# Gated decode kernel: the output projection matrix in runs of four rows, its operands from one transpose a group

## The chip, the cores and the metric

The kernel runs on one core of a Trainium2 chip. The metric is the device time of one execution in microseconds (us).

## The reference

One decode step of a gated mix of two branches, for a batch of 8 and a width of 576. Everything is bfloat16 at the edges.

```python
x = A_x                                             # [8, 1, 576]
g = sigmoid((x * gate_w).sum(-1, keepdims=True))    # one gate a batch row
# branch A: attention over the last W = 2048 positions of a cache of 8192
q = (x @ wq).reshape(B, 1, 32, 128).transpose(0, 2, 1, 3)
k = repeat(k_cache[:, :, Sk - W:, :], 2, axis=1)    # 16 K/V heads, two query heads each
v = repeat(v_cache[:, :, Sk - W:, :], 2, axis=1)
p = softmax(einsum("bhqd,bhkd->bhqk", q, k) * 128 ** -0.5)
a = einsum("bhqk,bhkd->bhqd", p, v).transpose(0, 2, 1, 3).reshape(B, 1, 4096) @ wo   # wo: [4096, 576]
# branch B: a channel MLP
b = gelu(layernorm(x) @ w1 + b1) @ w2 + b2          # w1: [576, 4608]
return g * a + (1 - g) * b
```

K and V are 2 x 8 x 16 x 2048 x 128 elements, 134 MB; all weights together are some 20 MB.

## The kernel before

**Planner.** The program is written as a list of operations, each with an engine, dependencies and a guessed cost. `schedule()` places them greedily by estimated start time and so fixes one order for each engine; `emit()` then writes that order with semaphore waits. What runs when on the chip is decided by those fixed orders and the waits. All large loads are issued by SP, in one order (`stream`): K units and V units in turn, a load of the projection matrix `wo` after each eighth V unit, and at the end the bias `b2` and the four chunks of `w2`. The loads land in nine slots of 16 KB a partition (`take_slot`, `slot_free`); SP waits until the work on a slot's old contents is done.

**Units and groups.** A group `g` is two K/V heads; there are 8. A unit is half a K/V head: four batch rows, 2048 positions, 2 MB. So a group has four K units and four V units (`q` = 0 to 3).

- `k_unit`: the load (L627), copies on POOL that lay the queries out as block matrices (L635), two 128x2048 transposes on DVE (L642), and QK matmuls on PE (L659 and, with the weights held, L173) into four PSUM banks.
- `softmax(g)` after the group's last K unit: maximum (L587) and small steps on DVE, four exponentials on ACT (L601), four transposes of the probabilities on DVE (L606). Then the row sums: the partial sum of each partition times the 32x32 identity `i32` (`dsum`, L610), a matmul with all ones (L611) that gives each partition all 32 sums in a row, the reciprocal (L613), and the product with the gate in the same layout (`rg`, L618).
- `v_unit`: the load (L675), sixteen PV matmuls on PE (L682) in four column groups, an evacuation on ACT to `EV` in f32 (L691), and four f32 matmuls (L697) that add up the parts: `EV` is the stationary operand (128 columns) and `i32` the moving one (8 columns). The result has the head dimension on partitions and 8 columns a unit. After each second unit ACT copies it out (`o32`, L707) and POOL multiplies by `rg` into `oT` (L715; for the last item DVE does it from PSUM).
- `wo_chunk`: a load of 8 heads of `wo` (L723), one row of 576 a partition and head, in a slot with a pitch of 768; then for each item two times two matmuls (L541) that add to the output accumulator in PSUM, columns 0 to 287 and 288 to 575 in two column groups.
- `m2_chunk`: `w2` (L746), the last chunk in three pieces; its matmuls add to the same accumulator by L541.

At the end DVE and ACT copy the accumulator out, half each (L764, L765), and SP and ACT store it (L767).

**Start.** Queries (L464, L466), the first MLP layer (L498, L500) and the gate's broadcast (L445) run before the first QK; POOL makes identities, masks and selection matrices in that time, and L404 is its one step in the layer norm.

Of the kernel before, what the change touches and what calls it, by code (L numbers as in the profile page):

```python
# [179 lines left out]
def build_kernel(nc, A_x, A_k_cache, A_v_cache, A_wq, A_wo, B_x, B_w1, B_b1, B_w2, B_b2, gate_w, out):  # L180
# [16 lines left out]
    WOP = 768  # L197
# [7 lines left out]
    with ExitStack() as es:  # L205
# [22 lines left out]
        req("i32", 32, F32)  # L228
        req("idf8", 8, F32)
# [19 lines left out]
        req("dsum", 32, F32)  # L249
        req("rr", 32, F32)  # L250
        req("rg", 2 * 32, F32)
        req("o32", 2 * 16, F32)
        req("EV", 2 * 512, F32)
        req("oT", Hkv * 16, BF)
# [54 lines left out]
        dsum = view("dsum")  # L309
        rr = view("rr")  # L310
        rg = view("rg").rearrange("p (g m) -> p g m", g=2)
        o32 = view("o32").rearrange("p (u m) -> p u m", u=2)
        oT = view("oT").rearrange("p (u h b) -> p u h b", u=Hkv, h=2)
# [20 lines left out]
        def col(i, parts=128):  # L334
            return cols[0:parts, i:i + 1]
# [23 lines left out]
        o_idf = add("pool", lambda e: e.tensor_copy(idf8, ident[0:8, 0:8]), deps=[o_ident], name="idf8", cost=0.15)  # L359
        o_nhalf = add("pool", lambda e: e.memset(col(C_NHALF, 8), -0.5), name="nhalf", cost=0.1)  # L360
# [79 lines left out]
        def b1ev_fn(e):  # L440
# [4 lines left out]
        o_gp = add("pe", lambda e: e.matmul(ps[:, BK_X, 384:400], ones_f[0:8, :], dg[:, 0:16], start=True, stop=True),  # L445
                   deps=[o_dga, o_dgb, o_onesf], name="g_pe", cost=0.4, after=[o_yTp])
        o_yT = add("dve", ev_T(yT, 1), deps=[o_gp, o_yTp], name="yT_ev", cost=0.2)
        o_gb = add("dve", lambda e: e.tensor_copy(gb, ps[:, BK_X, 384:400]), deps=[o_gp], name="gb_ev", cost=0.15)
        o_obh = add("dve", lambda e: e.tensor_copy(ob[:, 0:8], dg[:, 8:16]), deps=[o_dgb], name="ob_hi", cost=0.12)
# [4 lines left out]
        for q in range(4):  # L454
            o_i32.append(add("dve", (lambda q=q: lambda e: e.tensor_copy(i32[32 * q:32 * q + 32, :], ident[32 * q:32 * q + 32, 32 * q:32 * q + 32]))(),
                             deps=[o_ident, o_obl], name="i32_%d" % q, cost=0.15, prio=-1))

# [126 lines left out]
        def softmax(g):  # L584
# [25 lines left out]
            ds = add("dve", lambda e: e.tensor_scalar(out=dsum, in0=i32, scalar1=k(S), scalar2=None, op0=ALU.mult), deps=[s_] + o_i32 + ([rg_done[g - 1]] if g else []), name="ds_%d" % g, cost=0.16, prio=5)  # L610
            sp_ = add("pe", lambda e: e.matmul(ps[:, BK_S, 0:32], ones_f, dsum, start=True, stop=True), deps=[ds] + b6_r[-2:], after=b6_w[-1:], name="sum_pe%d" % g, cost=0.5, prio=5)  # L611
            b6_w.append(sp_)
            rc = add("dve", lambda e: e.reciprocal(out=rr, in_=ps[:, BK_S, 0:32]), deps=[sp_], name="rc_%d" % g, cost=0.16, prio=5)  # L613
            b6_r.append(rc)

            def rg_fn(e):
                in1 = bass.AP(arena_f, offset=foffs("gb"), ap=[[AST // 2, 128], [0, 2], [1, 8], [0, 2]])
                return e.tensor_tensor(out=rg[:, g % 2, :].rearrange("p (l b h) -> p l b h", l=2, b=8), in0=rr.rearrange("p (l b h) -> p l b h", l=2, b=8), in1=in1, op=ALU.mult)  # L618
            deps = [rc, o_gb]
            if g >= 2:  # L620
                deps.append(oT_done[2 * (g - 2) + 1])
            rg_done[g] = add("dve", rg_fn, deps=deps, name="rg_%d" % g, cost=0.16, prio=5)
# [48 lines left out]
        def v_unit(i):  # L671
# [21 lines left out]

            def us_fn(e):
                mm = None
                for r in range(4):
                    mm = e.matmul(ps[:, BK_S, OC + 16 * (item % 2) + 8 * (q % 2):OC + 16 * (item % 2) + 8 * (q % 2) + 8], EV[:, i % 2, 128 * r:128 * r + 128], i32[:, 8 * r:8 * r + 8],  # L697
                                  start=(r == 0), stop=(r == 3), skip_group_check=True)
                return mm
            u_sum[i] = add("pe", us_fn, deps=[u_ev[i]] + o_i32 + b6_r[-2:], after=b6_w[-1:], name="us%d" % i, cost=1.0, prio=3)  # L700
            b6_w.append(u_sum[i])
            if q % 2 == 1:
                hl = q // 2
                prev = u_sum[i]
                osrc = ps[:, BK_S, OC + 16 * (item % 2):OC + 16 * (item % 2) + 16]
                if item < Hkv - 1:
                    ev = add("act", lambda e: e.activation(out=o32[:, item % 2, :], in_=osrc, func=ACTF.Copy), deps=[prev] + ([oT_done[item - 2]] if item >= 2 else []), name="oev%d" % item, cost=0.25, prio=3)  # L707
                    o_item_ev[item] = ev
                    b6_r.append(ev)
                    eng, src_, deps = "pool", o32[:, item % 2, :], [ev, rg_done[g]]  # L710
                else:
                    eng, src_, deps = "dve", osrc, [prev, rg_done[g]]

                def om_fn(e):
                    return e.tensor_tensor(out=oT[:, item, :, :].rearrange("p h b -> p b h"), in0=src_.rearrange("p (b h) -> p b h", h=2),  # L715
                                           in1=rg[:, g % 2, 16 * hl:16 * hl + 16].rearrange("p (b h) -> p b h", h=2), op=ALU.mult)
                oT_done[item] = add(eng, om_fn, deps=deps, name="oT%d" % item, cost=0.25, prio=9)

        def wo_chunk(i):
            s = take_slot()  # L720
            h0 = WO_CH * i
            dst = slot(s)[:, 0:WO_CH * WOP].rearrange("p (t c) -> p t c", t=WO_CH)
            d = dma("sp", lambda e: e.dma_start(dst[:, :, 0:D], A_wo[128 * h0:128 * (h0 + WO_CH), :].rearrange("(t p) c -> p t c", p=128)),  # L723
                    "s%d" % s, WO_CH * 128 * D * 2, deps=slot_free[s], name="d_wo%d" % i, after=last_dma[-1:])
            last_dma.append(d)
            ops = []
            for item in range(h0 // 2, (h0 + WO_CH) // 2):
                mms = [(oT[:, item, h, :], dst[:, 2 * item + h - h0, 0:D]) for h in range(2)]
                ops.append(AccGroup("proj%d" % item, mms, [oT_done[item], d], cost=0.5).op)
            slot_free[s] = ops  # L730
# [107 lines left out]
```

## Time and profile before

| | |
|---|---|
| median of 3 runs | 369.37 us (369.34 to 369.59) |
| span of the profiled execution | 367.9 us (the page gives no other time for it) |
| PE, weight loads | 263.5 us busy (72%), 87.0 us (24%) |
| DVE | 210.4 us busy (57%) |
| ACT, POOL | 47.8 us (13%), 37.5 us (10%) |
| moved by DMA | 154.59 MB, 420 GB/s on average |

The profile is one execution, recorded by the hardware profiler. Its span runs from the first to the last instruction; the device time of a run is a little longer. Each row of a view names a source line (L697), an engine, an operation, its tiles and a count. PEld is the weight load of PE. A row of the timeline begins with start and duration in us, and ends with the idle time ahead of it and what ended that. "DMA to landing" is the time from the issue of a load by SP until its last byte has landed. The chain that ended last is followed back from the last instruction to what released it, step by step.

### The profile page before, as it was taken

How to read it: one execution, taken by the hardware profiler on the slowest of the kernel's cores; microseconds unless marked ns; L12 is line 12 of the kernel's file. 1: busy time of each engine (PE TensorE's matmuls, PEld its weight loads, DVE VectorE, ACT ScalarE, POOL GpSimd, SP SyncE). 2: the span in 40 equal slices, each digit the busy share in tenths (PEclk: the TensorE clock that was granted, in tenths of full speed). 3: DMA queues.
4: the chain of work that ended last, by engine and by line, in shares of the span. 5: the costliest groups of instructions: out<-in, count | busy, mean ns of one | idle time of the engine just before them, and what ended most of it. 6: DMA issues, size and time to landing. Idle time of an engine off the chain costs nothing.

```text
span 367.9 us, 4129 instructions
## 1 busy us (share of the span) xinstructions
PE 263.5 (72%) x1837; PEld 87.0 (24%) x1429; DVE 210.4 (57%) x253; ACT 47.8 (13%) x117; POOL 37.5 (10%) x163
## 2 busy tenths in 40 slices
PE   0349984797698589773986399774976398773984
PEld 0339200122132022110321032110321032113542
DVE  0704599699686665459654674469544775364000
ACT  1010000210300220003000310003100300003200
POOL 7020011012011002000101002010110000000000
PEclk9999999699599869887897869886996879886659
DMA  8999999999999999999999999999999999999994
GB/s 345 428 412 424 435 430 433 428 428 428 433 429 431 422 433 426 428 435 427 433 431 433 408 434 432 429 426 433 433 436 428 414 434 424 431 433 440 402 429 193
DMA packets 14923, 154.59 MB, mean 420 GB/s; under 512 B 1292, under 2 KB 5428, under 8 KB 6072
## 3 DMA queue, kind: packets, MB, share of 16 engines
q1 hardware_dynamic: 14848, 154.29, 98.9%
q8 instruction: 13, 0.21, 0.2%
q10 hardware_dynamic: 56, 0.03, 0.0%
q14 instruction: 6, 0.05, 0.0%
HBM read 154.31 MB, written 0.01 MB: 419 GB/s over the span
## 4 chain that ended last, share of the span: by engine, by line
DMA 61%; PE 20%; DVE 16%; SPq 1%; issue 1%; ACT 0%; DVEq 0%; ACTq 0%
DMA arena<-in_A_k_cache_dram 50%; DMA arena<-in_B_w_dram 11%; DVE arena L642 10%; PE ps L173 9%; PE ps L659 3%; DVE arena L587 3%; PE ps L498 2%; PE ps L682 2%; PE ps L697 2%; DVE arena L606 1%; DVE arena L590 1%; PE ps L500 1%; SPq L675 1%; DVE arena L596 0%; SPq L746 0%
## 5 line engine op out<-in xcount | busy, mean ns | idle before, releaser
L642 DVE STREAM_TRANSPOSE arena<-arena 128x2048 f32<-128x2048 f32 x64 | 145.5, 2299 | 71.1 <-DMA arena<-in_A_k_cache_dram 60.1
L173 PE MATMUL ps<-arena 128*128 128x512 bf16 x408 | 141.3, 462 | 0.0
L659 PE MATMUL ps<-arena 128*128 128x512 bf16 x128 | 58.8, 459 | 21.4 <-DVE arena L642 21.3
L691 ACT ACTIVATE arena<-ps 128x512 f32<-128x512 f32 x32 | 19.1, 598 | 196.8 <-PE ps L682 196.8
L659 PEld LDWEIGHTS ps<-arena 128*128 128x128 bf16 x128 | 15.0, 117 | 124.6 <-issue 71.3
L635 POOL COPY arena<-arena 32x32 bf16<-32x32 bf16 x128 | 26.0, 203 | 159.8 <-PE ps L173 145.2
L697 PE MATMUL ps<-arena 128*128 128x8 f32 x256 | 35.3, 269 | 8.7 <-ACT arena L691 7.7
L697 PEld LDWEIGHTS ps<-arena 128*128 128x128 f32 x256 | 34.0, 208 | 21.8 <-ACT arena L691 15.2
L682 PE MATMUL ps<-arena 128*32 128x512 bf16 x512 | 36.4, 410 | 2.9 <-DMA arena<-in_A_v_cache_dram 2.9
L651 PE MATMUL ps<-arena 128*128 128x512 bf16 x8 | 4.7, 585 | 40.8 <-DVE arena L606 40.8
L587 DVE TENSOR_REDUCE arena<-ps 128x1 f32<-128x2048 f32 x8 | 18.3, 2282 | 21.6 <-PE ps L173 21.6
L601 ACT ACTIVATE arena<-ps,arena 128x512 bf16<-128x512 f32 x32 | 21.6, 686 | 40.9 <-DVE arena L596 40.9
L606 DVE STREAM_TRANSPOSE arena<-arena 128x512 bf16<-128x512 bf16 x32 | 19.9, 674 | 0.9 <-ACT arena L601 0.9
L682 PEld LDWEIGHTS ps<-arena 128*32 128x32 bf16 x512 | 11.3, 100 | 37.4 <-issue 27.1
L715 POOL TENSOR_TENSOR arena<-arena 128x16 bf16<-128x16 f32 x15 | 4.0, 266 | 141.7 <-ACT arena L707 141.7
L498 PE MATMUL ps<-arena 128*128 128x8 bf16 x144 | 10.9, 201 | 4.7 <-DMA arena<-in_B_w_dram 4.7
L541 PE MATMUL ps<-arena 128*8 128x288 bf16 (+1 forms) x140 | 11.9, 316 | 2.9 <-DMA arena<-in_B_w_dram 2.8
L498 PEld LDWEIGHTS ps<-arena 128*128 128x128 bf16 x144 | 10.8, 157 | 5.2 <-DMA arena<-in_B_w_dram 5.2
L651 PEld LDWEIGHTS ps<-arena 128*128 128x128 bf16 x8 | 0.9, 107 | 45.1 <-DVE arena L606 45.1
L613 DVE RECIPROCAL arena<-ps 128x32 f32<-128x32 f32 x8 | 2.9, 358 | 13.9 <-PE ps L611 13.9
L420 PE MATMUL ps<-arena 8*128 8x8 bf16 x8 | 0.5, 167 | 13.4 <-DVE arena L393 9.7
L715 DVE TENSOR_TENSOR arena<-ps,arena 128x16 bf16<-128x16 f32 x1 | 0.2, 229 | 16.7 <-PE ps L697 16.7
(83 smaller groups left out, 97.1 us busy)
## 6 DMA issues: line engine op xcount, KB each, us to landing
arena<-in_A_k_cache_dram SPq DMA_DIRECT2D x32, 2048.0 KB, 33.3
arena<-in_A_v_cache_dram SPq DMA_DIRECT2D x32, 2048.0 KB, 34.1
arena<-in_B_w_dram SPq DMA_DIRECT2D x1, 4608.0 KB, 24.3
arena<-in_A_wo_dram SPq DMA_DIRECT2D x4, 1152.0 KB, 36.6
arena<-in_A_wq_dram SPq DMA_DIRECT2D x1, 4096.0 KB, 13.0
arena<-in_B_w_dram SPq DMA_DIRECT2D x3, 1296.0 KB, 14.8
arena<-in_B_w_dram SPq DMA_DIRECT2D x2, 576.0 KB, 20.6
arena<-in_A_wq_dram SPq DMA_DIRECT2D x1, 512.0 KB, 3.6
```

The lines of the kernel that those rows point to most:

```text
L173: return e.add_instruction(mybir.InstMatmult(name=nc.get_next_instruction_name(), engine=mybir.EngineType.PE, ins=[e.lower_ap(rhs), e.lowe ...
L498: ins = e.matmul(out_, lhsT, yT[:, kt, :], start=(kt == 0), stop=False)
L541: ins = e.matmul(ps[32 * j:32 * j + 8, BK_ACC, 0:JN], lhsT, rhs[:, JN * j:JN * j + JN], start=False, stop=True, skip_group_check=True, til ...
L587: mx = add("dve", lambda e: e.tensor_reduce(out=k(MX), in_=ps[:, 0:4, :].rearrange("p a n -> p (a n)"), axis=AXL.X, op=ALU.max), deps=[qk_ ...
L601: return e.activation(out=Pm[:, 512 * c:512 * c + 512], in_=ps[:, c, :], func=ACTF.Exp, bias=k(NB), scale=SCALE, accum_out=k(SUM + c))
L606: pts.append(add("dve", (lambda c=c: lambda e: e.transpose(bass.AP(arena, offset=aoffs("PT") + 2048 * (g % 2) + 128 * c, ap=[[AST, 128], [ ...
L635: return e.tensor_copy(dst, src)
L642: tr = add("dve", (lambda h=h, kb=kb: lambda e: e.transpose(bass.AP(arena_f, offset=foffs("KT") + kb * 2048, ap=[[AST // 2, 128], [1, 2048]]),
L659: mm = e.matmul(*args, start=False, stop=last) if rc == 0 else held_matmul(nc, e, *args, stop=last)
L682: mm = e.matmul(ps[c:c + 32, BK_OS[i % 2], :], PT[:, g % 2, 512 * q + 32 * t:512 * q + 32 * t + 32], slot(s)[:, 512 * t:512 * t + 512], st ...
L691: u_ev[i] = add("act", lambda e: e.activation(out=EV[:, i % 2, :], in_=ps[:, BK_OS[i % 2], :], func=ACTF.Copy), deps=[prev] + ([u_sum[i - ...
L697: mm = e.matmul(ps[:, BK_S, OC + 16 * (item % 2) + 8 * (q % 2):OC + 16 * (item % 2) + 8 * (q % 2) + 8], EV[:, i % 2, 128 * r:128 * r + 128 ...
```

## The change

Four matrix rows that lie together in `wo` now go to one partition. A load of 8 heads is two groups of 128 partitions x 4 rows: partition `p` of group `t` gets rows `4 p` to `4 p + 3`, 4608 B in one piece. The contraction of the projection is thereby split in another way: its 512 rows of a group (4 query heads x 128) are taken as `4 p + j`, with four matmul pairs for `j` = 0 to 3 in place of one pair a head.

The left operands have to follow. The sum of the units is turned round: a fixed selection matrix `selu` (64 columns) is stationary and `EV` (128 columns) moves, so that the result has query head and batch row on partitions (a block of 32 for each of the group's 4 heads, in it the 8 batch rows four times over) and the head dimension along the row. The row sums come from one matmul with a selection matrix `seln` and one moving column, so that each partition has its own sum; reciprocal and gate product are 128x1. ACT scales each partition while it copies the group out (`on`, bf16), and one 32x32-block transpose on DVE a group gives `oT` with `4 p + j` as the order. POOL builds `selu`, `seln` and `r8` once at the start, and one more small matmul gives the gate by partition (`gcol`).

Line numbers in the changed kernel: K transposes L663, QK L680, PV L703, evacuation L712, sums L721, row sums L638, reciprocal L640, gate product L642, scaling L727, group transpose L730, projection and MLP matmuls L569.

```diff
-            ds = add("dve", lambda e: e.tensor_scalar(out=dsum, in0=i32, scalar1=k(S), ...
-            sp_ = add("pe", lambda e: e.matmul(ps[:, BK_S, 0:32], ones_f, dsum, start=True, stop=True), ...
+            sp_ = add("pe", lambda e: e.matmul(ps[:, BK_S, 0:1], seln, k(S), start=True, stop=True), deps=[s_] + o_seln + ...
-            rc = add("dve", lambda e: e.reciprocal(out=rr, in_=ps[:, BK_S, 0:32]), ...
+            rc = add("dve", lambda e: e.reciprocal(out=rr, in_=ps[:, BK_S, 0:1]), ...
-            rg_done[g] = add("dve", rg_fn, deps=deps, name="rg_%d" % g, cost=0.16, prio=5)
+            rg_done[g] = add("dve", lambda e: e.tensor_tensor(out=rg[:, g % 2:g % 2 + 1], in0=rr, in1=gcol, op=ALU.mult), ...
...
+            hl = q // 2
+            osl = ps[64 * hl:64 * hl + 64, BK_S, OC + 128 * (g % 2):OC + 128 * (g % 2) + 128]
                 for r in range(4):
-                    mm = e.matmul(ps[:, BK_S, OC + 16 * (item % 2) + 8 * (q % 2):...], EV[:, i % 2, 128 * r:128 * r + 128], i32[:, 8 * r:8 * r + 8],
-                                  start=(r == 0), stop=(r == 3), skip_group_check=True)
+                    mm = e.matmul(osl, selu[:, r, q % 2, :], EV[:, i % 2, 128 * r:128 * r + 128],
+                                  start=(q % 2 == 0 and r == 0), stop=(q % 2 == 1 and r == 3), skip_group_check=True, tile_position=(0, 64 * hl))
...
-                    ev = add("act", lambda e: e.activation(out=o32[:, item % 2, :], in_=osrc, func=ACTF.Copy), ...
-                oT_done[item] = add(eng, om_fn, deps=deps, name="oT%d" % item, cost=0.25, prio=9)
+            if q == 3:
+                o_item_ev[g] = add("act", lambda e: e.activation(out=on[:, g % 2, :], in_=ps[:, BK_S, OC + 128 * (g % 2):OC + 128 * (g % 2) + 128], func=ACTF.Copy, scale=rg[:, g % 2:g % 2 + 1]), ...
+                oT_done[g] = add("dve", lambda e: e.transpose(bass.AP(arena, offset=aoffs("oT") + 128 * g, ap=[[AST, 128], [1, 128]]),
+                                                              bass.AP(arena, offset=aoffs("on") + 128 * (g % 2), ap=[[AST, 128], [1, WOR], [WOR, 32]])), ...
...
-            dst = slot(s)[:, 0:WO_CH * WOP].rearrange("p (t c) -> p t c", t=WO_CH)
-            d = dma("sp", lambda e: e.dma_start(dst[:, :, 0:D], A_wo[128 * h0:128 * (h0 + WO_CH), :].rearrange("(t p) c -> p t c", p=128)),
+            NT = WO_CH // WOR
+            dst = slot(s)[:, 0:WO_CH * D].rearrange("p (t j c) -> p t j c", t=NT, j=WOR)
+            d = dma("sp", lambda e: e.dma_start(slot(s)[:, 0:WO_CH * D].rearrange("p (t c) -> p t c", t=NT), A_wo[128 * h0:128 * (h0 + WO_CH), :].rearrange("(t p j) c -> p t (j c)", p=128, j=WOR)),
...
-            for item in range(h0 // 2, (h0 + WO_CH) // 2):
-                mms = [(oT[:, item, h, :], dst[:, 2 * item + h - h0, 0:D]) for h in range(2)]
+            for t in range(NT):
+                g = h0 // WOR + t
+                mms = [(oT[:, g, j, 0:8], dst[:, t, j, :]) for j in range(WOR)]
...
+        o_r8 = add("pool", lambda e: e.tensor_copy(r8..., ...idf8...), deps=[o_idf], name="r8", cost=0.2)
+        o_su0 = add("pool", lambda e: e.memset(view("selu"), 0.0), name="selu0", cost=0.5)
+        def g_fn(e):
+            e.matmul(ps[:, BK_X, 384:400], ones_f[0:8, :], dg[:, 0:16], start=True, stop=True)
+            return e.matmul(ps[:, BK_X, 400:401], r8, col(C_G, 8), start=True, stop=True)
+                    o_selu.append(add("pool", fn, deps=o_i32 + [o_su0], ...))     # 16 copies
+                o_seln.append(add("pool", fn, deps=o_i32, ...))                   # 4 copies
```

More of the change, by code (lines that the diff above doesn't have):

```diff
@@ L699, in us_fn @@
                 return mm
-            u_sum[i] = add("pe", us_fn, deps=[u_ev[i]] + o_i32 + b6_r[-2:], after=b6_w[-1:], name="us%d" % i, cost=1.0, prio=3)
+            u_sum[i] = add("pe", us_fn, deps=[u_ev[i]] + o_selu + b6_r[-2:], after=b6_w[-1:], name="us%d" % i, cost=1.0, prio=3)
             b6_w.append(u_sum[i])
[L702 to L716, printed above, removed]
-                oT_done[item] = add(eng, om_fn, deps=deps, name="oT%d" % item, cost=0.25, prio=9)
@@ new lines, in v_unit @@
+            if q == 3:
+                o_item_ev[g] = add("act", lambda e: e.activation(out=on[:, g % 2, :], in_=ps[:, BK_S, OC + 128 * (g % 2):OC + 128 * (g % 2) + 128], func=ACTF.Copy, scale=rg[:, g % 2:g % 2 + 1]),
+                                   deps=[u_sum[i], rg_done[g]] + ([oT_done[g - 2]] if g >= 2 else []), name="oev%d" % g, cost=0.3, prio=9)
+                b6_r.append(o_item_ev[g])
+                oT_done[g] = add("dve", lambda e: e.transpose(bass.AP(arena, offset=aoffs("oT") + 128 * g, ap=[[AST, 128], [1, 128]]),
+                                                              bass.AP(arena, offset=aoffs("on") + 128 * (g % 2), ap=[[AST, 128], [1, WOR], [WOR, 32]])),
+                                 deps=[o_item_ev[g]], name="oT%d" % g, cost=0.25, prio=9)
```

64 lines of the change are left out of this document (41 added, 23 removed).

## The prediction

> **What bounds the kernel now.** I read the page's span, DMA line and queue table first, then the chain that ended last, then busy time by stretch, and last the PE rows behind the final transfers.
>
> ```profile
> span 367.9 us, 4129 instructions
> ...
> DMA  8999999999999999999999999999999999999994
> ...
> DMA packets 14923, 154.59 MB, mean 420 GB/s; under 512 B 1292, under 2 KB 5428, under 8 KB 6072
> ...
> q1 hardware_dynamic: 14848, 154.29, 98.9%
> q8 instruction: 13, 0.21, 0.2%
> ...
> arena<-in_A_wo_dram SPq DMA_DIRECT2D x4, 1152.0 KB, 36.6
> ```
>
> The 16 DMA engines are at nine tenths or more in every slice but the first and the last: the kernel is a stream of 154 MB, and PE, DVE, ACT and POOL work beside it. The four loads of the output projection matrix are 4.7 MB of that stream. Each brings 8 heads x 128 rows of 576 bf16, so 1024 pieces of 1152 B; the four make 4096 of the 5428 packets under 2 KB. A load is listed 36.6 us before it lands: the queue is deep.
>
> ```profile
> 291.28 29.20 DMA arena<-in_A_k_cache_dram
> ...
> 348.46 16.55 DMA arena<-in_B_w_dram
> 365.02 0.04 issue
> 365.06 0.43 PE ps L541 x4
> ```
>
> In the chain the last K load lands at 320.5 (291.28 + 29.20) and the last piece of the second MLP matrix at 365.0. Four matmuls, the copy out and the store are all that follows. So what counts is how fast the bytes pass, and whether PE is ready when the last ones land.
>
> **The change, part by part.** Terms are taken off the profiled span of 367.9 us. The page gives no other time for that execution; the median of the runs, 369.37 us (369.34 to 369.59), is 1.47 us above it, and I leave that gap as it is.
>
> *The transfers.* Columns below: stretch, its length, busy time of PE, weight loads, DVE, ACT and POOL, PE clock, DMA share, GB/s.
>
> ```profile
> 140.00:200.00 60.00, 43.42 (x269) 11.62 (x189) 35.72 (x33) 6.93 (x17) 6.49 (x31) 0.86 1.01 431
> 220.00:285.00 65.00, 49.14 (x286) 12.64 (x196) 37.77 (x33) 7.11 (x18) 6.74 (x32) 0.85 1.01 431
> 124.00:138.00 14.00, 7.87 (x46) 2.64 (x33) 10.68 (x22) 3.98 (x10) 0.21 (x1) 0.76 1.02 421
> 205.00:219.00 14.00, 7.88 (x50) 2.04 (x36) 11.39 (x21) 3.68 (x10) 0.81 (x4) 0.76 1.03 422
> 286.00:300.00 14.00, 7.87 (x46) 1.70 (x37) 11.32 (x21) 3.38 (x9) 0.82 (x4) 0.76 1.03 424
> ```
>
> The first two stretches carry K and V only, in pieces of 16 KB, at 431 GB/s. The other three hold one projection load each and run at 421, 422 and 424. Lost against 431: 14 x (10, 9 and 7)/431 = 0.32, 0.29 and 0.23 us, 0.28 on average. I put that loss to the number of pieces. Per DMA engine a load is 64 pieces of 1152 B, where 73.7 KB in 16 KB pieces would be 4.5; so 0.28 us / 59.5 = 4.7 ns a piece. After the change an engine moves 16 pieces of 4608 B a load (four matrix rows that lie together, for one partition): 48 fewer, 48 x 4.7 ns = 0.226 us a load, **0.90 us for four**. The ends: the rounding of the rates puts a piece between 3.9 and 5.5 ns, so 0.75 to 1.06 us; all of the loss would be 4 x 0.28 = 1.1 us, nothing at all if the loss has another cause than the count. I take 0.90, since the pieces are the one thing that sets these stretches apart.
>
> [...]
>
> *The DMA queue.*
>
> ```profile
> 95.74 0.59 SPq L723 DMA_DIRECT2D arena<-in_A_wo_dram  x1
> 107.98 18.53 SPq L627 DMA_DIRECT2D arena<-in_A_k_cache_dram  x1
> ...
> DMA to landing us min/median/max: 20.1/33.3/40.5
> DVE arena L642 <- DMA arena<-in_A_k_cache_dram: 60.1, 15, 10.5
> ```
>
> The K load behind a projection load takes 18.53 us to issue where that load itself took 0.59; with a quarter of the pieces ahead of it I expect that hold to go. That buys nothing: the shortest way of a K load from issue to landing is 20.1 us (third row), so the engines never ran out of work. Cost 0.
>
> *The sums on PE.*
>
> ```profile
> L697 PE MATMUL ps<-arena 128*128 128x8 f32 x48 | 9.3, 327 | 1.9 <-ACT arena L691 1.4 <-DVE arena L613 0.5
> L541 PE MATMUL ps<-arena 128*8 128x288 bf16 (+1 forms) x92 | 8.4, 331 | 2.9 <-DMA arena<-in_B_w_dram 2.8
> ...
> 337.48 3.49 PEld L697 LDWEIGHTS ps<-arena 128*128 128x128 f32 x16 [0.65 <-issue]
> 337.51 3.55 PE L697 MATMUL ps<-arena 128*128 128x8 f32 x16 [0.54 <-DVE arena L613]
> 340.99 3.38 PE L682 MATMUL ps<-arena 128*32 128x512 bf16 x32
> ...
> 344.30 1.95 PE L697 MATMUL ps<-arena 128*128 128x8 f32 x16
> ...
> L697 PE MATMUL ps<-arena x256: 170/256/382, 76.3 to 353.8; 128*128 128x8 f32 x128
> L611 PE MATMUL ps<-arena x16: 190/273/419, 71.3 to 336.6; 128*128 128x32 f32 x16
> ```
>
> A unit's sum is four f32 matmuls, eight instructions. Today 128 columns are loaded as weights and 8 are streamed; sixteen instructions take 3.55 us at the low clock and 1.95 at the high one, so 0.222 or 0.122 each, and weight load and matmul span the same time. The change turns this round: 64 columns are loaded, 128 streamed. A streamed column costs (190 - 170)/24 = 0.83 ns at best and (419 - 382)/24 = 1.54 ns at worst (last two rows: 32 columns against 8), so 128 cost 0.107 or 0.197 us, and half a load 0.061 or 0.111. If the load hides behind the matmul ahead of it, an instruction costs the larger, 0.107 or 0.197: PE gains a little, nothing lost. If it does not, 0.168 or 0.308. I take the hidden case, because in the two L697 rows that start at 337.5 loads and matmuls lie over each other for all 3.5 us.
>
> Over the span this is beside the DMA. Where it could matter is the tail: after 325 us six units are summed in 9.3 us, and the last matmuls (second row) wait 2.8 us for transfers. That is PE's slack. It grows by the softmax steps that go, and shrinks by the one projection load that falls after the last K landing (0.23):
>
> ```profile
> L691 ACT ACTIVATE arena<-ps 128x512 f32<-128x512 f32 x32 | 19.1, 598 | 196.8 <-PE ps L682 196.8
> L707 ACT ACTIVATE arena<-ps 128x16 f32<-128x16 f32 x15 | 2.8, 184 | 29.6 <-PE ps L697 29.6
> L606 DVE STREAM_TRANSPOSE arena<-arena 128x512 bf16<-128x512 bf16 x32 | 19.9, 674 | 0.9 <-ACT arena L601 0.9
> L610 DVE TENSOR_SCALAR arena<-arena 128x32 f32<-128x32 f32 x8 | 1.9, 242 | 0.3
> L613 DVE RECIPROCAL arena<-ps 128x32 f32<-128x32 f32 x8 | 2.9, 358 | 13.9 <-PE ps L611 13.9
> ```
>
> The multiply at L610 goes (0.24) and the reciprocal reads one column instead of 32 (some 0.2 less). At the very end a group's scaling on ACT comes to about 0.28 us (between 184 ns for 16 columns and 598 for 512) and the transpose to 0.17 to 0.67 (a quarter of L606, or all of it); before, one DVE multiply stood there. Eight matmuls of the group before run meanwhile. I book 0.4 against 0.4: slack stays 2.8 - 0.2, or 2.6 us. The projection itself stays at 64 matmul pairs of the same shape.
>
> *The new wait on DVE.* A group's products were formed on POOL; now DVE stands before the group's 128x128 transpose until ACT has scaled the sums, with K transposes queued behind it, then QK on PE, then SP, which waits for the slot. Each of the seven waits inside the stream is bounded by one evacuation, one sum and one scaling, 0.6 + 1.8 + 0.3 = 2.7 us, and below by nothing. I book 0: DVE stands 60 us waiting for K landings anyway (last row of the queue's fence), and the DMA queue behind it is 20 us deep or more. Without that cover it would be up to 7 x 2.7 = 19 us.
>
> *The start.* Twenty small copies, a copy into a broadcast matrix and a memset join POOL; one f32 matmul joins PE.
>
> ```profile
> 14.75 0.56 POOL L404 TENSOR_TENSOR arena<-arena 8x1 f32<-8x1 f32 x1 [7.12 <-DVE arena L403]
> 24.12 4.12 POOL L635 COPY arena<-arena 32x32 bf16<-32x32 bf16 x16 [8.82 <-ACT arena L483]
> PE ps L498 <- DMA arena<-in_B_w_dram: 4.7, 1, 4.7
> ```
>
> Twenty copies at 4.12/16 = 0.26 us are 5.2 us inside an idle stretch of 8.82; the memset and the broadcast go ahead of a wait of 7.12; PE waits 4.7 us for the first MLP matrix after the queries. Cost 0; if a selection copy spilled past its cover, some 0.3 us on work that the queue hides too.
>
> Sum: 367.9 - 0.90 = 367.0 us of span, **368.5 us** with the 1.47. What a measurement of this kernel can tell is about 0.2%, 0.74 us.
>
> **The rivals.**
> *PE's tail becomes the end (slower).* If weight loads stand in line and the sums stay at the low clock, six units cost 6 x 8 x 0.308 = 14.8 us, 5.5 more than 9.3. Less the 2.6 of slack, the end comes 2.9 us after the forecast: 371.4. It decides from about 9.3 + 2.6 + 0.9 + 0.7 = 13.5 us for the six. For it: the same sixteen instructions show both rates within 10 us. Against it: overlapping loads, and 32 PV matmuls in 3.38 us, eight sets of four in 0.42 each with all their loads inside. [...]
>
> *The engines end apart (either sign).*
>
> ```profile
> 362.00:363.00 1.00, 1.00 (x18) 0.65 (x18) 0.00 (x0) 0.00 (x0) 0.00 (x0) 1.00 0.66 257
> 363.00:364.00 1.00, 0.85 (x12) 0.27 (x8) 0.00 (x0) 0.00 (x0) 0.00 (x0) 1.00 0.38 141
> 364.00:365.00 1.00, 0.54 (x6) 0.18 (x6) 0.00 (x0) 0.00 (x0) 0.00 (x0) 1.00 0.13 48
> ```
>
> The engines finish over some three microseconds, and the slowest sets the end. One of the 13 instruction packets (16 KB, 0.6 us at 431/16 GB/s) on another engine moves the end by 0.6 us: 369.1, or 367.9. For it: the new program has other lengths. Against it: it has about as many instructions.
>
> *The rows do not come as longer pieces, or the loss was not theirs:* 369.4. Against it: source and destination are both 4608 B in one run.
>
> **How the numbers follow.** Forecast 0.60 (its own range 368.2 to 368.7; 0.14 of it under 0.2%); engines apart 0.22, half each way (0.08 faster, 0.14 the same); PE's tail 0.12, slower; no effect 0.06 (0.04 the same, 0.02 slower). Faster 0.46 + 0.08 = 0.54, same 0.14 + 0.14 + 0.04 = 0.32, slower 0.14. The range runs from 367.7, the earlier end with 0.2 to spare, to 369.6, no effect with as much; it leaves out the tail rival.
>
> **What would show it.** Packets fall by 3072 to about 11850, those under 2 KB by 4096 to about 1330. Stretches with a projection load rise to about 429 GB/s. The K issue behind such a load falls to some 0.6 us. The six last sums stay near 9 us, and the last matmuls still wait for transfers by 2 us or more. Wrong: a last PE group that no longer waits for a DMA, a DMA share under 0.9 before 360 us, or a rate at the projection loads that stays at 422.

## Result, and the profile after

| | before | after |
|---|---|---|
| median of 21 runs each, same chip | 369.48 us (369.28 to 369.71) | 368.67 us (368.48 to 369.43) |
| ratio | | 0.9982 [0.9976, 0.9988] |
| profiled execution | span 367.9 us | 369.14 us, span 367.4 us |

The change gains 0.81 us by the medians. The ratio lies near that of the means, 368.83 against 369.49 us, a gain of 0.65. After's 21 executions lie in two groups: 13 at 368.48 to 368.69 us with a mean granted clock of 0.882 to 0.896, and 8 at 369.10 to 369.43 with 0.870 to 0.879. Before's 21 do not split. The profiled execution of after, 369.14 us, is one of the later group, so its tail must be read as that of the eight. What makes the two groups is the one thing that the forecast lacked.

The page of after (span, DMA share in 40 slices, packets):

```profile
span 367.4 us, 4082 instructions
...
DMA  8999999999999999999999999999999999999994
...
DMA packets 11850, 154.58 MB, mean 421 GB/s; under 512 B 1292, under 2 KB 1332, under 8 KB 3000
```

3073 packets are gone, and those under 2 KB are down by 4096, as forecast; the bytes are the same to 0.01 MB. The DMA engines are still at nine tenths or more in every slice but the first and the last. The same five stretches of after (length, busy time of PE, weight loads, DVE, ACT, POOL, PE clock, DMA share, GB/s):

```profile
140.00:200.00 60.00, 43.13 (x255) 10.73 (x180) 35.85 (x33) 6.74 (x15) 4.91 (x24) 0.86 1.01 430
220.00:285.00 65.00, 45.88 (x295) 12.40 (x215) 36.81 (x34) 7.71 (x17) 5.73 (x28) 0.90 1.01 430
124.00:138.00 14.00, 8.69 (x53) 2.50 (x39) 9.28 (x21) 2.99 (x9) 0.82 (x4) 0.76 1.01 428
205.00:219.00 14.00, 7.62 (x40) 2.19 (x22) 11.52 (x21) 3.38 (x9) 0.67 (x4) 0.76 1.02 430
286.00:300.00 14.00, 7.61 (x38) 1.78 (x25) 11.05 (x21) 3.38 (x9) 0.82 (x4) 0.76 1.00 426
```

With a projection load the rate was 421, 422 and 424; it is now 428, 430 and 426, near the 430 of K and V alone. SP's queue of after, the landing of K loads, and two waits of DVE:

```profile
96.22 0.59 SPq L739 DMA_DIRECT2D arena<-in_A_wo_dram  x1
108.31 0.54 SPq L648 DMA_DIRECT2D arena<-in_A_k_cache_dram  x1
...
DMA to landing us min/median/max: 25.1/34.5/42.5
...
DVE arena L663 <- DMA arena<-in_A_k_cache_dram: 57.2, 16, 10.0
DVE arena L730 <- ACT arena L727: 25.9, 7, 11.4
```

The K issue behind a projection load takes 0.54 us instead of 18.53. The new wait on DVE (last row: sum, times, longest) is 25.9 us in seven; a K load takes 25.1 us or more from issue to landing. Groups of PE after 325 us, then its timeline there:

```profile
L721 PE MATMUL ps<-arena 128*64 128x128 f32 x48 | 8.4, 342 | 1.8 <-ACT arena L712 1.4 <-DVE arena L640 0.4
L569 PE MATMUL ps<-arena 128*8 128x288 bf16 (+1 forms) x92 | 10.2, 396 | 2.6 <-DMA arena<-in_B_w_dram 2.6
```

```profile
336.76 3.64 PE L721 MATMUL ps<-arena 128*64 128x128 f32 x16 [0.35 <-DVE arena L640]
342.30 1.96 PE L721 MATMUL ps<-arena 128*64 128x128 f32 x16
352.16 3.74 PE L569 MATMUL ps<-arena 128*8 128x288 bf16 x38
357.74 2.33 PE L569 MATMUL ps<-arena 128*8 128x288 bf16 x18 [1.84 <-DMA arena<-in_B_w_dram]
360.85 4.15 PE L569 MATMUL ps<-arena 128*8 128x288 bf16 x36 [0.78 <-DMA arena<-in_B_w_dram]
```

Sixteen turned-round instructions take 3.64 and 1.96 us (3.55 and 1.95 before), the six sums 8.4 us (9.3). The last two rows are the surprise. Beside them the same matmuls of before:

```profile
354.14 4.29 PE L541 MATMUL ps<-arena 128*8 128x288 bf16 x38
358.83 1.27 PE L541 MATMUL ps<-arena 128*8 128x288 bf16 x18 [0.40 <-DMA arena<-in_B_w_dram]
361.93 2.01 PE L541 MATMUL ps<-arena 128*8 128x288 bf16 x26 [1.82 <-DMA arena<-in_B_w_dram]
364.34 0.54 PE L541 MATMUL ps<-arena 128*8 128x288 bf16 x6 [0.41 <-DMA arena<-in_B_w_dram]
365.06 0.41 PE L541 MATMUL ps<-arena 128*8 128x288 bf16 x4 [0.18 <-DMA arena<-in_B_w_dram]
```

After takes 2.33 us for the 18 where before took 1.27, and 4.15 us for the last 36 with no wait inside, where before waited three times for transfers. The chain that ended last says the same:

```profile
282.49 36.96 DMA arena<-in_A_k_cache_dram
...
329.05 31.75 DMA arena<-in_B_w_dram
...
360.85 4.17 PE ps L569 x36
```

Before, it held transfers until 365.02 and then four matmuls. In this execution it leaves the transfers at 360.8, and PE sets the end.

### The profile page after: what moved, and what is told of

It is laid out like the page before. It is cut to its first block, busy times and chain, and to the rows that moved or that the text cites. A ratio compares the mean times of both kernels' runs of the same rounds, so it can differ in the third digit from the quotient of the medians.

```text
span 367.4 us, 4082 instructions
## 1 busy us (share of the span) xinstructions
PE 255.2 (69%) x1817; PEld 83.4 (23%) x1431; DVE 208.7 (57%) x253; ACT 48.0 (13%) x110; POOL 37.3 (10%) x170
## 4 chain that ended last, share of the span: by engine, by line
DMA 67%; PE 17%; DVE 13%; issue 1%; ACT 1%; SPq 1%; DVEq 0%; ACTq 0%
DMA arena<-in_A_k_cache_dram 51%; DMA arena<-in_B_w_dram 15%; DVE arena L663 11%; PE ps L173 8%; PE ps L526 2%; PE ps L680 2%; PE ps L569 1%; DVE arena L615 1%; PE ps L721 1%; PE ps L703 1%; ACT arena L629 1%; PE ps L528 1%; DVE arena L624 0%; DVE arena L618 0%; SPq L395 0%
## 5 line engine op out<-in xcount | busy, mean ns | idle before, releaser
L663 DVE STREAM_TRANSPOSE arena<-arena 128x2048 f32<-128x2048 f32 x64 | 145.3, 2296 | 62.9 <-DMA arena<-in_A_k_cache_dram 57.2
L173 PE MATMUL ps<-arena 128*128 128x512 bf16 x402 | 135.5, 448 | 17.7 <-DVE arena L663 10.4
L680 PE MATMUL ps<-arena 128*128 128x512 bf16 x114 | 51.5, 452 | 13.3 <-DVE arena L663 13.3
L712 ACT ACTIVATE arena<-ps 128x512 f32<-128x512 f32 x32 | 19.2, 599 | 203.8 <-PE ps L703 203.8
L721 PE MATMUL ps<-arena 128*64 128x128 f32 x256 | 36.5, 291 | 9.6 <-ACT arena L712 7.7
L680 PEld LDWEIGHTS ps<-arena 128*128 128x128 bf16 x128 | 13.9, 109 | 120.5 <-issue 67.9
L703 PE MATMUL ps<-arena 128*32 128x512 bf16 x512 | 34.1, 382 | 3.3 <-DMA arena<-in_A_v_cache_dram 3.3
L721 PEld LDWEIGHTS ps<-arena 128*64 128x64 f32 x256 | 29.2, 144 | 25.4 <-ACT arena L712 14.0
L672 PE MATMUL ps<-arena 128*128 128x512 bf16 x6 | 3.5, 586 | 37.9 <-DVE arena L634 31.8
L703 PEld LDWEIGHTS ps<-arena 128*32 128x32 bf16 x512 | 11.4, 96 | 39.4 <-issue 26.4
L730 DVE STREAM_TRANSPOSE arena<-arena 128x128 bf16<-128x128 bf16 x8 | 2.6, 319 | 26.0 <-ACT arena L727 25.9
L569 PE MATMUL ps<-arena 128*8 128x288 bf16 (+1 forms) x140 | 14.1, 358 | 2.6 <-DMA arena<-in_B_w_dram 2.6
L526 PEld LDWEIGHTS ps<-arena 128*128 128x128 bf16 x144 | 10.8, 159 | 4.7 <-DMA arena<-in_B_w_dram 4.7
L672 PEld LDWEIGHTS ps<-arena 128*128 128x128 bf16 x8 | 0.9, 107 | 46.1 <-DVE arena L634 39.5
L569 PEld LDWEIGHTS ps<-arena 128*8 128x8 bf16 (+1 forms) x140 | 6.7, 102 | 12.5 <-issue 4.2
L640 DVE RECIPROCAL arena<-ps 128x1 f32<-128x1 f32 x8 | 1.4, 169 | 13.9 <-PE ps L638 13.9
## 6 DMA issues: line engine op xcount, KB each, us to landing
arena<-in_A_k_cache_dram SPq DMA_DIRECT2D x32, 2048.0 KB, 34.5
```

The lines of the kernel that those rows point to most:

```text
L173: return e.add_instruction(mybir.InstMatmult(name=nc.get_next_instruction_name(), engine=mybir.EngineType.PE, ins=[e.lower_ap(rhs), e.lowe ...
L526: ins = e.matmul(out_, lhsT, yT[:, kt, :], start=(kt == 0), stop=False)
L569: ins = e.matmul(ps[32 * j:32 * j + 8, BK_ACC, 0:JN], lhsT, rhs[:, JN * j:JN * j + JN], start=False, stop=True, skip_group_check=True, til ...
L663: tr = add("dve", (lambda h=h, kb=kb: lambda e: e.transpose(bass.AP(arena_f, offset=foffs("KT") + kb * 2048, ap=[[AST // 2, 128], [1, 2048]]),
L680: mm = e.matmul(*args, start=False, stop=last) if rc == 0 else held_matmul(nc, e, *args, stop=last)
L703: mm = e.matmul(ps[c:c + 32, BK_OS[i % 2], :], PT[:, g % 2, 512 * q + 32 * t:512 * q + 32 * t + 32], slot(s)[:, 512 * t:512 * t + 512], st ...
```

## The experiments

Theory: the gain is the number of pieces, and PE's clock over the last matmuls takes part of it back in some executions. Rivals: the gain comes from the sums and the softmax steps, or from where a piece begins in memory, or the new waits cost something. All times are medians; before's in the same comparison stands in brackets.

**The pieces alone.** The kernel before with four-row pieces, all else as it was.

```diff
-            dst = slot(s)[:, 0:WO_CH * WOP].rearrange("p (t c) -> p t c", t=WO_CH)
-            d = dma("sp", lambda e: e.dma_start(dst[:, :, 0:D], A_wo[...].rearrange("(t p) c -> p t c", p=128)),
+            dst = slot(s)[:, 0:WO_CH * D].rearrange("p (t c) -> p t c", t=WO_CH)
+            d = dma("sp", lambda e: e.dma_start(slot(s)[:, 0:WO_CH * D].rearrange("p (t c) -> p t c", t=2), A_wo[...].rearrange("(t p j) c -> p t (j c)", p=128, j=4)),
```

> The kernel before with one thing changed: a load of the projection matrix comes in pieces of four rows (4608 B). The sums, softmax and scaling stay as before, so the projection multiplies rows and operands that do not belong together; only its time is read. Theory (number of pieces): 48 pieces fewer an engine and load at 4.7 ns, 0.90 us for four loads: 368.6 us against 369.5 for before, stretches with a projection load at 429 GB/s instead of 421 to 424, the K load behind one issues in about 0.6 us instead of 18. Rival (the gain of the change comes from its compute part): 369.5, no change.

368.61 us (368.48 to 368.72, 8 runs) [369.50]; ratio 0.9975 [0.9965, 0.9985]. Run once more it gave 368.53 (368.36 to 368.85, 8 runs) [369.54], 0.9974 [0.9964, 0.9984]. So 0.89 and 1.01 us, and no second group.

> The runs-only kernel with pieces of four rows once more, as the partner of the eight-row one and of the kernel before with filled tail: 368.6 us.

Stretches and the end of PE in the first of the two:

```profile
124.00:138.00 14.00, 8.95 (x50) 3.23 (x39) 9.79 (x22) 3.57 (x10) 0.27 (x1) 0.76 1.01 431
205.00:219.00 14.00, 8.24 (x46) 3.19 (x38) 10.83 (x22) 3.66 (x10) 0.00 (x0) 0.76 1.01 428
286.00:300.00 14.00, 7.87 (x48) 2.43 (x31) 10.94 (x22) 3.98 (x10) 0.41 (x2) 0.76 1.00 424
```

```profile
355.77 7.05 PE L541 MATMUL ps<-arena 128*8 128x288 bf16 x82
363.27 1.08 PE L541 MATMUL ps<-arena 128*8 128x288 bf16 x10 [0.45 <-DMA arena<-in_B_w_dram]
```

The whole gain is there without any of the arithmetic of the change, and the last ten matmuls still wait for a transfer. A rate over 14 us is coarse, though: in the third stretch the second run of the same program had 433 GB/s where this one has 424.

The packet records of the traces are finer. They give each packet's end, so the packets of the load queue (q1), added up, tell when the same number of bytes had landed in two kernels. Against before's profile, four-row pieces gain 0.23 us at each of the four projection loads in both runs of this kernel, and over the K and V loads between them the difference moves by 0.02 us at most. The kernel after gains 0.24, 0.22, 0.22 and 0.28 us; the 0.05 more at the last also stands in the kernel with the arithmetic alone (next), which gains 0.01 us at most at the others. So the transfers gain at these loads and not between them, and 0.23 us / 48 is 4.8 ns a piece.

**The arithmetic alone.** The kernel after with one-row pieces again.

```diff
-            d = dma("sp", ... slot(s)[:, 0:WO_CH * D].rearrange("p (t c) -> p t c", t=NT), A_wo[...].rearrange("(t p j) c -> p t (j c)", p=128, j=WOR)),
+            d = dma("sp", ... slot(s)[:, 0:WO_CH * D].rearrange("p (t c) -> p t c", t=WO_CH), A_wo[...].rearrange("(t p) c -> p t c", p=128)),
```

> The changed kernel with one thing undone: a load of the projection matrix comes in pieces of one row (1152 B) again; turned sums, scaling by partition and transposes stay. Rows and operands of the projection do not belong together; only the time is read. Theory (number of pieces): 369.5 us, as before, stretches with a projection load at 421 to 424 GB/s, the K load behind one held for some 18 us again. Rival (compute part): 368.6, the whole gain without the pieces. Second rival (the compute part costs, the pieces gain more than 0.9): over 369.7.

369.89 us (369.27 to 370.36, 11 runs) [369.50]; ratio 1.0012 [1.0003, 1.0021]. In its profile the rate and the hold of the K issue are back:

```profile
107.80 18.24 SPq L648 DMA_DIRECT2D arena<-in_A_k_cache_dram  x1
```

```profile
124.00:138.00 14.00, 8.70 (x53) 2.51 (x39) 9.12 (x20) 3.38 (x9) 0.82 (x4) 0.76 1.02 421
```

So the arithmetic gains nothing; it costs 0.4 us, which the forecast had put at nothing and only the second rival of this run had named. The profiled execution was the shortest of the eleven, so its rows do not show where the cost lies. The next two kernels narrow it down.

**PE kept busy before the last chunks.** The kernel after, and the kernel with the arithmetic alone, each with six matmuls on constants ahead of the second chunk of `w2` and four ahead of the third.

```diff
+    WARM = {1: 6, 2: 4}
+                if ci in WARM:
+                    def warm(e, k=WARM[ci]):
+                        for _ in range(k):
+                            ins = e.matmul(ps[:, 0, :], ident, maskR, start=True, stop=True)
+                        return ins
+                    o_m2.append(add("pe", warm, deps=exp_done[NG - 1], ..., after=o_m2[-1:] + [pv_last[NG - 1]]))
```

> The changed kernel with ten matmuls more on PE that nobody reads (128x512, identity times a constant mask, into a free bank): six ahead of the second chunk of the second MLP matrix, four ahead of the third, where PE otherwise waits for transfers. Eight of 21 executions of the changed kernel took 369.1 to 369.4 us at a mean granted clock up to 0.879, the others 368.5 to 368.7 at 0.882 and more. Theory (clock): in those eight PE is granted half its clock over the last matmuls and is later than the last transfer; with the gaps filled the clock stays up, all executions take 368.4 to 368.7, and the last group of matmuls waits for a transfer. Rival (the DMA engines end further apart in some executions): a third of the executions still take 369.1 to 369.4. Second rival (the filling itself delays the last matmuls): 369 and more in all.

> The sums-only kernel (turned sums, pieces of one row; the projection's rows and operands do not belong together, only the time is read) with the ten matmuls that nobody reads ahead of the second and third chunk of the second MLP matrix. The sums-only kernel took 369.3 to 370.4 us, median 369.9, where before took 369.5. Theory (its excess is PE's clock over the last matmuls): 369.3 to 369.6 us, as narrow as before. Rival (the excess lies elsewhere, in transfers or waits): median 369.9 again, and as wide.

With the change: 368.55 us (368.43 to 368.87, 8 runs) [369.50], 0.9975 [0.9965, 0.9985]. With the arithmetic alone: 369.45 (369.29 to 369.59, 11 runs) [369.48], 0.9999 [0.9990, 1.0008]. No execution of the first lies above 368.87, where 8 of 21 did without the filling, and the 0.4 us of the second are gone: nine of its eleven executions without the filling were later than all eleven with it. The mean clocks of these two sets overlap, however (0.873 to 0.888 without, 0.879 to 0.888 with), so that this cost is PE's clock is argued from what removes it. The end of PE with the change and the filling, where L771 is the filling:

```profile
357.18 1.24 PE L771 MATMUL ps<-arena 128*128 128x512 bf16 x5 [0.16 <-issue]
358.35 1.27 PE L570 MATMUL ps<-arena 128*8 128x288 bf16 x18
359.56 1.04 PE L771 MATMUL ps<-arena 128*128 128x512 bf16 x4
361.03 1.88 PE L570 MATMUL ps<-arena 128*8 128x288 bf16 x26 [0.44 <-DMA arena<-in_B_w_dram]
363.36 1.09 PE L570 MATMUL ps<-arena 128*8 128x288 bf16 x10 [0.44 <-DMA arena<-in_B_w_dram]
```

The 18 take 1.27 us and the last 36 wait twice for transfers: the DMA sets the end. What the filling does is shown by the times: this one profiled execution need not have lost its clock without it, since its clock changes, at 349.42 and 356.25 us, lie within 0.1 us of those of an execution of after that kept it (below). Between the two filled kernels only the pieces differ: 369.45 - 368.55 = 0.90 us, though they ran in two comparisons.

**The kernel after once more**, unchanged, for a profile of the earlier group.

> The changed kernel once more, beside the others on one chip. Theory (clock): two groups of executions again, near 368.6 and near 369.2 us, the later one with the lower mean clock. Rival (the first measurement's later group belongs to its chip): one group near 368.6.

368.66 us (368.44 to 369.37, 11 runs) [369.48], 0.9982 [0.9973, 0.9991]; 7 at 368.44 to 368.73 with a clock of 0.882 to 0.893, 4 at 368.96 to 369.37 with 0.875 to 0.882, so here the two groups touch in clock. Its profiled execution (368.55 us, clock 0.888) is of the earlier group:

```profile
352.85 4.18 PE L569 MATMUL ps<-arena 128*8 128x288 bf16 x38
357.75 1.27 PE L569 MATMUL ps<-arena 128*8 128x288 bf16 x18 [0.72 <-DMA arena<-in_B_w_dram]
360.87 2.03 PE L569 MATMUL ps<-arena 128*8 128x288 bf16 x26 [1.84 <-DMA arena<-in_B_w_dram]
363.35 1.08 PE L569 MATMUL ps<-arena 128*8 128x288 bf16 x10 [0.46 <-DMA arena<-in_B_w_dram]
```

The same program, starting the 18 at 357.75 against 357.74: 1.27 us here, 2.33 there, and then 26 in 2.03 and a wait where the other has 36 in 4.15 and none. What differs is the granted clock (the third column from the right). First the profile of after, then this one, in stretches of 1 us:

```profile
350.00:351.00 1.00, 0.46 (x4) 0.46 (x5) 0.00 (x0) 0.49 (x1) 0.00 (x0) 0.93 1.02 430
...
354.00:355.00 1.00, 0.98 (x15) 0.36 (x12) 0.00 (x0) 0.00 (x0) 0.00 (x0) 0.86 1.10 467
355.00:356.00 1.00, 0.90 (x16) 0.45 (x10) 0.00 (x0) 0.00 (x0) 0.00 (x0) 1.00 1.00 425
356.00:357.00 1.00, 0.00 (x0) 0.00 (x0) 0.00 (x0) 0.00 (x0) 0.00 (x0) 1.00 1.02 435
357.00:358.00 1.00, 0.26 (x4) 0.15 (x6) 0.00 (x0) 0.00 (x0) 0.00 (x0) 0.85 0.97 410
...
364.00:365.00 1.00, 1.00 (x12) 0.41 (x8) 0.00 (x0) 0.00 (x0) 0.00 (x0) 0.74 0.00 0
```

```profile
349.00:350.00 1.00, 1.00 (x16) 0.21 (x8) 0.00 (x0) 0.00 (x0) 0.00 (x0) 0.66 1.05 441
...
356.00:357.00 1.00, 1.00 (x16) 0.47 (x11) 0.00 (x0) 0.00 (x0) 0.00 (x0) 0.93 1.07 456
```

The clock is 1.00 or 0.50 in the rows between, so a mixed value tells when it changed: 0.93 in 350 to 351, going down, is 0.14 us at half, so 350.86. In the same way after changes at 350.86 (down), 354.28 (up), 357.70 (down) and 364.52 (up), the other at 349.32 (down) and 356.14 (up). These points lie 3.42, 3.42 and 6.82 us apart, and 6.82: always whole steps of 3.41. The steps of the two executions lie 1.54 us apart. In after the step from 354.28 to 357.70 takes in nearly all of the 1.84 us wait and only 1.60 us of matmuls, and the clock falls at its end, right as the 18 begin. In the other the step from 356.14 to 359.55 has 0.89 + 1.27 = 2.16 us of matmuls and the next one 2.03, and the clock stays. So in these two it is where the steps happen to lie against PE's waits.

**The filling on the kernel before.**

```diff
+    WARM = {1: 6, 2: 4}
+                if ci in WARM:
...
```

> The kernel before with the ten matmuls that nobody reads in the tail. Theory (before ends with its last transfer, whatever PE's clock): 369.5 us, no change. Rival (the filling helps any kernel): 369.3 or less; second rival (it delays the last matmuls): over 369.7.

369.70 us (369.43 to 371.14, 12 runs) [369.54]; 1.0009 [1.0000, 1.0018]. No gain, and two of the twelve are late, as the second rival has it. The profiled execution is one of these two (371.01; the other is 371.14):

```profile
356.52 4.40 PE L542 MATMUL ps<-arena 128*8 128x288 bf16 x38
361.08 1.24 PE L754 MATMUL ps<-arena 128*128 128x512 bf16 x5 [0.16 <-issue]
...
364.42 2.37 PE L542 MATMUL ps<-arena 128*8 128x288 bf16 x36
```

There the 38 start 2.4 us later than in before's profile (354.14): sixteen sums ahead of them, at 344.19, took 3.58 us at the low clock (0.50) where before's took 1.95 (at 1.00). The filling then stands in the way of matmuls whose data are there: the last 36 run without a wait. Here the filling took 0.44 us off a tail that waits (369.89 to 369.45) and nothing off this one, which is late.

**Half-row pieces.** The kernel before with 576 B pieces, twice as many.

```diff
-            d = dma("sp", lambda e: e.dma_start(dst[:, :, 0:D], A_wo[...].rearrange("(t p) c -> p t c", p=128)),
+            dst = slot(s)[:, 0:WO_CH * D].rearrange("p (k t c) -> p k t c", k=NJ, t=WO_CH)
+            d = dma("sp", lambda e: e.dma_start(dst, A_wo[...].rearrange("(t p) (k c) -> p k t c", p=128, k=NJ)),
```

> The kernel before with the projection matrix loaded in half rows (576 B, the two halves of the columns apart in the slot): 128 pieces an engine and load instead of 64, same bytes, same matmuls. Theory (number of pieces, 4.7 ns each): 64 x 4.7 = 0.30 us a load, 1.2 us in all, 370.7 us; stretches of 14 us with a projection load at about 413 GB/s. [...] Second rival (pieces do not matter): 369.5.

371.43 us (371.16 to 371.93, 5 runs) [369.50]; ratio 1.0054 [1.0041, 1.0066]: 1.93 us lost, 1.5 to 2.4 by the interval, where the count said 1.2. So the price does not hold here: 1.93 us / 256 is 7.5 ns a piece. By the landed bytes the four loads lose 0.48, 0.41, 0.71 and 0.50 us where the count said 0.30 each. A stretch of this kernel with a projection load alone in flight:

```profile
129.50:130.50 1.00, 1.00 (x4) 0.15 (x1) 1.00 (x2) 0.00 (x0) 0.00 (x0) 0.50 1.12 355
```

At 355/16 GB/s a piece of 576 B takes 26.0 ns, at 431/16 it would take 21.4. That is 4.6 ns a piece, but the stretch is a chosen one: from 293 to 294 us, where the third load ends, the rate was 332 GB/s, and from 294 to 295 it was 340. Some 0.7 us, 0.2 a load, lie beyond the count. The third load, the costliest, has a K issue behind it that SP could not get rid of for 27 us:

```profile
266.49 27.09 SPq L627 DMA_DIRECT2D arena<-in_A_k_cache_dram  x1
```

Whether that hold is the cause wasn't tried. Where the pieces start is a rival: counted from the matrix's start, half of them start 64 or 192 B off a boundary of 256 B, which no projection load of the other kernels does. The next two kernels test 128 B alone, so it stays open.

**Where a piece begins.** The kernel before, its projection loads replaced by pieces of 1152 B at a pitch of 1280 B from the K cache: all on a boundary of 256 B, or all 128 B off it. Of the matrix rows, counted from the matrix's start, every second one starts 128 B off.

```diff
+            d = dma("sp", ... A_k_cache[0, i, 0:5120, :].rearrange("(t p f) d -> p t (f d)", p=128, f=5)[:, :, 0:D]),
...
+            d = dma("sp", ... [:, :, 64:64 + D]),
```

> The kernel before, with the four projection loads replaced by loads of as many pieces of 1152 B (1024 a load) from an unused part of the K cache, a piece each 1280 B, so that every piece starts on a 256 B boundary; the projection matrix is left out, only the time is read. Theory A (a piece costs 4.7 ns wherever it starts): 369.5 us, as before. [...]

> As the aligned kernel, but every piece starts 128 B off a 256 B boundary. Theory A (count only): 369.5 us, the same as the aligned one. [...]

369.49 and 369.51 us (11 runs each) [369.48]; ratios 1.0000 [0.9991, 1.0008] and 1.0002 [0.9993, 1.0011]. Neither differs from the kernel before, nor from the other, and by the landed bytes no load of either gains or loses more than 0.02 us. So a start 128 B off costs nothing that can be seen here.

**Eight-row pieces.** The pieces-only kernel with one run of 9216 B a partition.

```diff
+            d = dma("sp", lambda e: e.dma_start(slot(s)[:, 0:WO_CH * D], A_wo[...].rearrange("(p j) c -> p (j c)", p=128)),
```

> The runs-only kernel (before with the projection loads in longer pieces; rows and operands of the projection do not belong together, only the time is read), now with pieces of eight rows, 9216 B. Theory (4.7 ns a piece): 8 pieces fewer an engine and load than with four rows, 0.15 us in all: 0.15 below the four-row kernel of the same call, about 368.45 us. Rival (at 4608 B nothing is left to gain): the same as the four-row kernel.

368.37 us (368.31 to 368.54, 5 runs) [369.54]; 0.9969 [0.9957, 0.9981], 0.16 below four-row pieces in the same comparison, where eight pieces fewer an engine and load came to 0.15. The intervals of the two overlap, so the times agree rather than prove. By the landed bytes the loads gain 0.26 to 0.28 us each on before, where four-row pieces gain 0.23: 0.26 us / 56 pieces is 4.6 ns. This kernel is the shortest of all here. The turned-round sums with eight-row pieces and the filling weren't tried.

## Why the prediction was right, and where it was not

Forecast 368.5 us in 367.7 to 369.6, measured 368.67.

1. **The pieces: right in cause, and in size down to 1152 B.** 0.90 us forecast. Measured 0.89, 1.01 and, between the two filled kernels, 0.90; at each load 0.23 us where 0.226 was forecast. That the size came out so close has luck in it: it was worked out from rates 7 to 10 GB/s apart, and one program's rate over such a stretch differs by 9 GB/s between two runs. The price of a piece, 4.7 ns, held at 4608 and 9216 B (4.8 and 4.6 ns), and not at 576 B (7.5 ns). The upper end of the forecast's own range, 368.7, takes a gain of 0.67 us from 369.37, or 0.17 a load, which no run shows: the intervals of both runs of the pieces alone, 0.55 to 1.29 and 0.59 to 1.33 us, hold 0.67, but the 0.23 us at each load are more than 0.17. What makes up the 4.7 ns of a piece isn't shown. A start 128 B off a boundary of 256 B showed no cost: 369.51 us against 369.49.
2. **The K issue: right.** 18.53 us became 0.54, and K landings came no sooner (34.5 us in the median against 33.3). The gain fits the pieces without it: eight-row pieces gain another 0.03 to 0.05 us a load over four-row ones, with which the first of these K issues already takes 0.54 us.
3. **The sums: right that weight loads stay hidden, not that PE gains a little.** Sixteen instructions in 3.64 and 1.96 us are 0.228 and 0.123 each, nearer to the hidden case (0.197 and 0.107) than to loads in line (0.308 and 0.168), and no less than before's 0.222 and 0.122. The six sums' 8.4 us against 9.3 come from the clock: eight instructions took 1.09 us at the high clock in after where before's took 1.88 at the low one.
4. **The tail's slack: the step that failed.** It was booked as "slack stays 2.8 - 0.2, or 2.6 us", all of it at the rate that the last matmuls of before had. The wait is there (2.6 us in the after row), but in the profiled execution the work behind it ran at half the rate: 18 + 36 matmuls in 2.33 + 4.15 = 6.48 us against 1.27 + 2.03 + 1.08 = 4.38 in the other profile of the same program. That is 2.1 us more work and brings PE past the last transfer. In 12 of 32 executions of after (8 of 21, 4 of 11) the time is longer, by 0.68 us in the median of the eight (369.26). The median of the thirteen others in the first comparison is 368.58, a gain of 0.90, which is what the pieces are worth. The forecast had named the sign, a last PE group that no longer waits for a DMA, but gave no price to PE's clock over the last matmuls.
5. **The rival of PE's tail** had the place right and the mechanism wrong: loads in line would have shown in the sixteen sums and did not (0.228 and 0.123 us an instruction, where 0.308 and 0.168 were booked for them). Its price was wrong too: 371.4 against 369.1 to 369.4.
6. **The waits of DVE: cost right, one bound too low.** The seven waits are 25.9 us, but two of them, 4.04 and 11.45 us, lie behind the last K load, where nothing is queued behind DVE. DVE's timeline of after, the longest wait inside the stream and the longest of all:

```profile
305.82 0.31 DVE L730 STREAM_TRANSPOSE arena<-arena 128x128 bf16<-128x128 bf16 x1 [3.63 <-ACT arena L727]
...
352.66 0.31 DVE L730 STREAM_TRANSPOSE arena<-arena 128x128 bf16<-128x128 bf16 x1 [11.45 <-ACT arena L727]
```

   The five inside the stream come to 25.9 - 15.5 = 10.4 us, under the 19 of the bound, though two of them are 3.34 and 3.63 us where 2.7 was the most for each. The DMA queue covers them: K loads are 25.1 us or more from landing, and the filled kernel with the arithmetic alone is at 369.45 [369.48].
7. **Small steps.** The transpose is 0.31 us and the reciprocal 0.17 where 0.17 to 0.67 and 0.16 were booked; the start shows no cost in the same kernel. Engines that end apart were not needed to explain anything, and not tried. The 1.47 us between the span and the time was a median's against one execution's span: after's own profiled execution has 369.14 - 367.4 = 1.74.

What is shown of point 4: the two clocks in two profiles of one program, and that with the filling both the later group of after and the 0.4 us of the arithmetic alone are gone. The first rests on eight executions; with 12 late ones in 32, eight in time would come up by chance in some 2 of 100 cases. That the clock changes in steps of 3.41 us holds in all thirteen profiles: in stretches of 1 us after 325 us the changes of each lie on one grid to within 0.03 us, and the grids lie at different places against the start. How busy PE must be in a step is not settled. After 350 us the clock fell after steps with up to 1.6 us of matmuls (after, 354.28 to 357.70: 1.60) and stayed after those with 1.74 or more (the arithmetic alone, 357.06 to 360.47). But in before's profile it fell at 347.42, after a step in which PE was busy for 3.22 us with sums and PV matmuls, so busy time alone is not the rule. Nothing was run that moves the steps. Why they lie at other places in another execution isn't shown.

Why the kernel before does not split was not tried by itself. In the two profiles of the pieces alone PE works without a pause from 355.77 and 354.49 to 362.8, which leaves no such step. Before's own profile does have waits of 0.40 and 1.82 us; its steps there hold 2.04 and 2.07 us of matmuls, and its clock stays. With the sums turned round the first 38 projection matmuls begin at 352.16 and 352.85 us in the two profiles of after, against 354.14 before, so PE is done with them sooner, and it waits 1.84 and 0.72 us for `w2` behind them, against 0.40 before. Whether that is why only after splits stays open.

## What to carry to other kernels

Here, with the DMA engines at nine tenths or more from end to end, each piece cost time beside its bytes (4.7 ns an engine from 1152 B up, 7.5 ns at 576 B), and a longer run was worth its count even above 1 KB (0.23 us a load with 4608 B, 0.26 to 0.28 with 9216 B); check it by one kernel that changes the runs alone. Price a tail that waits for the last transfers at both clocks of PE, here 1.00 and 0.50: the same 18 matmuls took 2.33 us behind a wait of 1.84 us in one execution and 1.27 behind one of 0.72 in another, and before, whose matmuls ahead of them began 1.3 to 2.0 us later, waited 0.40 there. Cheap matmuls in the waits held the rate (368.55 us and none late of eight executions), but not where PE came late to them (369.70 us, two late of twelve).

## What the runs showed of the hardware that was not expected

- The same 18 matmuls took 1.27 or 2.33 us in two executions of one program, starting within 0.01 us of each other; the granted clock changed only in whole steps of 3.41 us, and the grids of the two lay 1.54 us apart.
- A K issue on SP behind one of the first three projection loads was held 18.24 to 22.29 us where the load has 64 pieces an engine (before, and the arithmetic alone), 23.00 and 27.09 us with 128, and not at all with 16 (0.53 to 0.54 us).
- One program's 14 us stretch showed 424 and 433 GB/s in two runs: a rate over one load is good to some 2%. When the same bytes have landed repeats to 0.02 us between loads, and showed 0.23 us at each of the four.
